# Product 2 by seven inner products in later gate/up, attention-output and down pairs, with h blocks handed on by a list of holders

## The chip, the core and the metric

The kernel runs on one core of one Trainium2 chip. The core has TensorE (matmuls into the eight banks of PSUM), VectorE and ScalarE (element-wise work on SBUF and PSUM), GpSimd (here only set-up and small powers) and SyncE, whose queue issues every DMA. The metric is the time of one execution on the device in microseconds, the median of the runs shown; lower is better.

## What is computed

One transformer-like block with a linear attention branch and a SwiGLU branch, for 2048 tokens of width 1024 and an inner width of 3584, all inputs in bf16:

```
xn  = layernorm(x)
q, k, v = split(xn @ wqkv)                      # 32 heads of 32
pq, pk  = phi(q), phi(k)                        # phi(t) = (t > 0 ? t + 1 : exp(t)) + 1e-6
kv, z   = sum_s pk v^T, sum_s pk                # per head
s   = ((pq @ kv) / (pq . z + 1e-6)) @ wo
g   = silu((silu(xn @ w_gate) * (xn @ w_up)) @ w_down)
out = x + s * g
```

## The kernel before

**Products.** A large matrix product is cut into 2 x 2 blocks and computed by the Strassen-Winograd scheme: seven block products (numbered 1 to 7) in place of eight, with sums of operand blocks made by VectorE beforehand and sums of results made afterwards. The stationary operand (a 128-column slice of weights or of tokens) has the combinations 5, 6, 7 and 3, made by `sums` (line 958); the moving operand has T1 to T4. One *set* (class `Set`, line 487) is one such scheme for one slice: its `step(m)` issues product m as wide matmuls (128 x 512 output, one PSUM bank), four of them where the half contraction is 512 long, fourteen in the down projection. Two sets that share their moving operand form a *pair* (class `Pair`, line 589).

Products 1 and 5 of a pair's two sets are computed together by a *joint* (class `Joint`, line 551): the same scheme applied once more inside, as seven inner products of narrow matmuls (128 x 256 output), two per inner product, seven in the down projection. A joint has four parts a, b, c, d; it takes two PSUM banks x and y, has ScalarE copy part of y to x and to a buffer of `q_ring`, and has VectorE add in parts b and c. Its end calls `put1` or `put5`: `put1` lets ScalarE copy the finished product 1 into a second bank, so that product 2 can accumulate onto one copy (result (0,0)) and product 6 onto the other; `put5` lets ScalarE copy product 5 into `s5_ring`. Product 6 is followed by a 512-wide VectorE add into a third bank, product 7 by one into `d_ring`. A first pair of a stage has no joint and runs `HEAD`, then `TAIL`; pairs with joints are interleaved with the rest of the pair before them in the fixed order `LINK` (line 607), issued by `feed` (line 610).

**Stages.** In order of time: layernorm, k and v with the kv sums (to about 100 us); the q, gate and up blocks in the order of `order` (line 1390), each 512 columns wide, for the token halves p = 0 and 1, one pair each (`q_pair`, `gu_pair`); after ("u", 3) four attention-output pairs (`s_pair`, line 1221); after ("u", 6) the down projection in four groups of 512 tokens (class `Group`, line 1308, and the loop at 1469), the first without joints. The element-wise product h goes through DRAM (`h_scr`) and comes back in blocks; a group's blocks (0,0), (0,1), (1,1), (1,0), their sums 5 and 6 (7 and 3 overwrite blocks), and the inner sums of joints 1 and 5 live in nine slots of 7 KB (`hslots`), handed on by callbacks `first` to `sixth` at named steps.

**Weights.** `wload` (line 968) brings a block of 1 MB into one of two slots of `raw_ring`, makes its sums into `cmb_ring`, and has `inner_stat` (line 995) make the inner sums of operands 1 and 5 into `in_ring`. `inner_move` (line 1022) makes the inner combinations of the moving operand once per token half.

**Order.** Everything above only records operations in a `Plan` (line 31) with the regions they read and write, in units of 256 bytes. `Plan.schedule` then orders them per engine by assumed costs and due times; TensorE may take an operation out of order among the next `WINDOW` = 6 matmul groups. `emit` writes the queues with semaphore waits. Each engine runs its queue in order.

Lines 229, 359, 369 and 372 are the helpers for matmuls, ScalarE operations, VectorE two-operand operations and DMA issue, so most groups of the profile carry these lines; tiles tell them apart (W: weights and inner sums; H: blocks of many kinds; X, P: the normalised tokens' halves; TM: small buffers; ps: PSUM).

Of the kernel before, what the change touches and what calls it, by code (L numbers as in the profile page):

```python
# [239 lines left out]
def build_kernel(nc, A_x, A_wqkv, A_wo, B_w_gate, B_w_up, B_w_down, out, WINDOW=6, NWARM=14, NPE=4, LEAD=12.0):  # L240
# [12 lines left out]
    with ExitStack() as es:  # L253
# [178 lines left out]
        d_ring = Ring(TM, 4 * KB, 2 * KB, 2)  # L432
# [5 lines left out]
        x_ring = Ring(W, 36 * KB, 2 * KB, 4)  # L438
        xn_ring = Ring(W, 0, 2 * KB, 2)
        xs_ring = Ring(W, 44 * KB, 4 * KB, 2)  # L440
# [46 lines left out]
        class Set:  # L487
# [4 lines left out]
            def __init__(self, ops, evac, dring):  # L492
                self.ops, self.evac, self.dring, self.direct = ops, evac, dring, None
# [19 lines left out]

            def put5(self, e):
                self.s5 = s5_ring.take()
                act([bank_r[e]], [self.s5.r], self.s5.ap(F32), ps[e][:, :], ACT.Identity)
                bfree(e)

            def step(self, m):
# [11 lines left out]
                elif m == 6:  # L531
                    self.grp(6, self.b, False)
                    self.c = balloc()
                    tt([bank_r[self.b], self.s5.r], [bank_r[self.c]], ps[self.c][:, :], ps[self.b][:, :],
                       self.s5.ap(F32), ALU.add)
                elif m == 7:
                    self.grp(7, self.b, False)
                    if self.direct is not None:
                        self.direct(1, 1, self.b, self.s5)
                        return  # L540
                    d = self.dring.take()
                    tt([bank_r[self.b], self.s5.r], [d.r], d.ap(F32), ps[self.b][:, :], self.s5.ap(F32), ALU.add)
# [46 lines left out]
        class Pair:  # L589
# [3 lines left out]
            def __init__(self, s0, s1, joint, at):  # L593
                self.sets, self.joint, self.at = (s0, s1), joint, at

            def do(self, w):
                if w[0] == "j":
# [4 lines left out]
                for fn in self.at.get(w, ()):  # L602
                    fn()

        HEAD = "1_0 5_0 1_1 2_0 5_1 6_0 2_1 6_1".split()
        TAIL = "7_0 3_0 7_1 4_0 3_1 4_1".split()
        LINK = "7_0 nj1a 3_0 7_1 nj1b nj5a 3_1 nj1c nj5b 4_0 nj1d nj5c 4_1 n2_0 nj5d n6_0 n2_1 n6_1".split()
        last_pair = [None]

        def feed(pair):  # L610

            prev = last_pair[0]
            if pair is None or not pair.joint:
                if prev is not None:
                    for w in TAIL:
                        prev.do(w)
# [3 lines left out]
            else:  # L620
                for w in LINK:
                    if w[0] == "n":
                        pair.do(w[1:])
                    elif prev is not None:
# [197 lines left out]
        def kv_set(u, w, stat):  # L822
# [16 lines left out]
            st = Set(ops, evac, d_ring)  # L839
# [118 lines left out]
        def sums(A, o, rd, wr):  # L958

            tt(rd, [wr[0]], o[0], A[0, 1], A[1, 1], ALU.add, True)  # L960
            tt(rd + [wr[0]], [wr[1]], o[1], o[0], A[0, 0], ALU.subtract, True)
            tt(rd, [wr[2]], o[2], A[0, 0], A[0, 1], ALU.subtract, True)
            tt(rd + [wr[1]], [wr[3]], o[3], A[1, 0], o[1], ALU.subtract, True)
# [4 lines left out]
        def wload(src, joint):  # L968
# [6 lines left out]
            cv = c.ap(FP16).rearrange("p (m w kt n) -> p m w kt n", m=4, w=2, n=128)  # L975
            cr = [c.sub(q * 2 * KB, 2 * KB).r for q in range(4)]
            sums({(k, i): v[:, :, 4 * k:4 * k + 4, i * 128:i * 128 + 128] for k in range(2) for i in range(2)},
                 [cv[:, q] for q in range(4)], [s.r], cr)

            def whole(m):  # L980
                if m in RAW_OF:
                    k, i = RAW_OF[m]
                    return v[:, :, 4 * k:4 * k + 4, i * 128:i * 128 + 128], s.r
                return cv[:, SUM_OF[m]], cr[SUM_OF[m]]

            def block(m):
                bl, r = whole(m)
                return (lambda k0, n, i: bl[:, i, k0:k0 + n, :]), r

            def stat(w, m):  # L990
                bl, r = whole(m)
                return [bl[:, w, q, :] for q in range(4)], r
            return stat, inner_stat(block, joint, 4, in_ring.take)

        def inner_stat(block, joint, kt, take):

            inner = {}
            for m in joint:
                bl, r = block(m)
                t = take()  # L1000
                n = kt // 2 * 256
                tv = t.ap(FP16, 0, 4 * n).rearrange("p (m kt n) -> p m kt n", m=4, n=128)
                tr = [t.sub(q * n, n).r for q in range(4)]
                A = {(k, i): bl(k * (kt // 2), kt // 2, i) for k in range(2) for i in range(2)}
                sums(A, [tv[:, q] for q in range(4)], [r], tr)
                inner[m] = (A, r, tv, tr)

            def jstat(m, k):
                A, r, tv, tr = inner[m]
                if k in RAW_OF:  # L1010
                    return [A[RAW_OF[k]][:, q, :] for q in range(kt // 2)], r
                return [tv[:, SUM_OF[k], q, :] for q in range(kt // 2)], tr[SUM_OF[k]]
            return jstat

        def xset(stat, w, xv, evac, dring):
# [4 lines left out]
            return Set(ops, evac, dring)  # L1020

        def inner_move(v, kt, at, raw=False, ms=(1, 5)):
# [3 lines left out]
            for m, places in zip(ms, at):  # L1026
# [3 lines left out]
                if raw and m == 1:  # L1030
# [9 lines left out]
        def in_places(arena, base, n):  # L1040
            return tuple(tuple((arena, base + (3 * m + q) * n) for q in range(3)) for m in range(2))
# [3 lines left out]
        def joint_of(jstat, xin, n, s0, s1):  # L1045
            def ops(m):
                def f(k):
# [4 lines left out]
            return {"1": Joint(ops(1), lambda w, b: (s0, s1)[w].put1(b)),  # L1052
                    "5": Joint(ops(5), lambda w, b: (s0, s1)[w].put5(b))}
# [17 lines left out]
        def q_load(s):  # L1071
            return wload(wqkv_v[:, :, s * 512:(s + 1) * 512], (1, 5))
# [10 lines left out]
        def q_pair(p, s, stats, at):  # L1083
            stat, jstat = stats

            def evac(w):
                def f(i, j, ap, r, bank):
                    g = 2 * (2 * s + w) + i
                    o, orr = pq_tile(p, g, j)
                    phi_evac(ap, r, o, orr, "ps" if bank is not None else "sb", i == 0)  # L1090
                return f
            s0, s1 = (xset(stat, w, XV[p], evac(w), d_ring) for w in range(2))
# [50 lines left out]
        def gu_load(k, n):  # L1143
            return wload((wg_v if k == "g" else wu_v)[:, :, n * 512:(n + 1) * 512], (1, 5))
# [13 lines left out]
        def gu_pair(p, kind, n, stats, at):  # L1158
# [38 lines left out]
            s0, s1 = (xset(stat, w, XV[p], (ev_g if kind == "g" else ev_u)(w), d_ring) for w in range(2))  # L1197
# [5 lines left out]
        def blocks(get, kt):  # L1203

            def block(m):
                ap, r = get(m)
                return (lambda k0, n, i: ap[:, k0:k0 + n, 128 * i:128 * i + 128]), r

            def stat(w, m):
                ap, r = get(m)  # L1210
                return [ap[:, q, 128 * w:128 * w + 128] for q in range(kt)], r
            return block, stat

        so_ring = Places([(TM, o * KB) for o in (8, 9, 12, 13)] + [(H, o * KB) for o in range(32, 40)], 1 * KB)
# [6 lines left out]
        def s_pair(g):  # L1221
            p, j0 = g // 2, g % 2
            A = {}
            for k in range(2):
                o = pq_off(p, k, j0)
                for i in range(2):
                    A[k, i] = (H.at(o, 4 * KB, FP16).rearrange("p (q t) -> p q t", t=512)[:, :, 256 * i:256 * i + 256],
                               H.reg(o, 4 * KB))
            c = ss_ring.take()
            cv = c.ap(FP16).rearrange("p (m q t) -> p m q t", m=4, t=256)  # L1230
            cr = [c.sub(q * 2 * KB, 2 * KB).r for q in range(4)]
            sums({q: a for q, (a, _) in A.items()}, [cv[:, q] for q in range(4)], [A[0, 0][1], A[1, 0][1]], cr)

            def get(m):
                return A[RAW_OF[m]] if m in RAW_OF else (cv[:, SUM_OF[m]], cr[SUM_OF[m]])
# [10 lines left out]
            s0, s1 = (xset(stat, w, MV, evac(w), d_ring) for w in range(2))  # L1246
            return Pair(s0, s1, joint_of(inner_stat(block, (1, 5), 4, in_ring.take), MIN, 2, s0, s1), {})
# [4 lines left out]
        def dblock(*at):  # L1252

            if len(at) == 1:
# [8 lines left out]
              "T4": dblock((W, 12 * KB), (H, 0))}  # L1263
# [21 lines left out]
        DAT = (tuple((W, q * 3584) for q in range(3)), ((W, 28 * KB), (W, 28 * KB + 3584), (W, 43 * KB)))  # L1285

        class Slots:
# [8 lines left out]
            def give(self, s):  # L1296
                self.free.append(s.k)

        hslots = Slots([(X, 0), (X, 7 * KB), (X, 14 * KB), (X, 21 * KB), (W, 20 * KB), (W, 36 * KB),
                        (H, 7 * KB), (H, 14 * KB), (H, 21 * KB)], 7 * KB)  # L1300
        g_ring = Places([(W, o * KB) for o in (47, 48, 49, 50)], 1 * KB)
        sl_ring = Places([(W, o * KB) for o in (51, 27, 35, 19)], 1 * KB)
        xo_ring = Places([(TM, 8 * KB), (TM, 9 * KB), (TM, 12 * KB), (TM, 13 * KB), (W, 11 * KB)], 1 * KB)
# [4 lines left out]
        class Group:  # L1308


            def __init__(self, g, cuts):
                self.g, self.cuts = g, cuts
                self.s, self.j = {}, {}

            def load(self, k, i):
                s = self.s[k, i] = hslots.take()
# [10 lines left out]
            def sum5(self):  # L1327
                self.s[5] = hslots.take()
                self.mk(self.s[5], self.s[0, 1], self.s[1, 1], ALU.add)

            def sum67(self):
                self.s[6] = hslots.take()
                self.mk(self.s[6], self.s[5], self.s[0, 0], ALU.subtract)
# [250 lines left out]
```

## Time and profile before

| | |
|---|---|
| median of 3 runs | 717.33 us (717.17 to 718.4) |
| the profiled execution's own time | 716.87 us |
| its span, first to last instruction | 715.1 us |
| granted TensorE clock | 0.998 |
| HBM read and written | 61.87 MB and 23.20 MB |

The span is the time in which the profile shows instructions; the execution's own time also has what lies before the first and after the last. Busy times of the page's first part are unions of the recorded intervals of an engine. A matmul's recorded end is modelled and overlaps the next one's start. A group's row gives its count, its busy time, the mean duration of one in ns, and the idle time of the engine ahead of it with what ended it.

### The profile page before, as it was taken

What the parts mean: (1) busy time and instruction counts of PE and PEld (TensorE: products, weight loads), DVE (VectorE), ACT (ScalarE), POOL (GpSimd) and SP (SyncE); (2) the same over time, 40 slices, a digit from 0 to 9 for tenths busy, and PEclk for the clock granted to TensorE, in tenths of its full rate; (3) what the DMA queues carried; (4) which work ended last, traced back from release to release, by engine and by line L of the source; (5) the groups of instructions that cost most, each with busy time, mean ns of one, the idle gap of its engine ahead of it and who ended that gap; (6) DMA issues with size and microseconds to landing.
All of it is one profiled execution on the core that took longest, in us unless ns stands there. A gap on an engine that the chain in (4) does not pass through costs nothing.

```text
span 715.1 us, 10861 instructions
## 1 busy us (share of the span) xinstructions
PE 705.0 (99%) x4035; PEld 385.8 (54%) x4064; DVE 528.0 (74%) x1181; ACT 407.4 (57%) x785; POOL 13.7 (2%) x35
## 2 busy tenths in 40 slices
PE   8999999999999999999999999999999999999997
PEld 3444445555555555555555555555554465565643
DVE  6998998676976797678998455957659994737442
ACT  4776655877876786679966665565662122121211
POOL 2111000000000000000000000000000000000000
PEclk9999999999999999999999999999999999999999
DMA  9443213113211330274225227554336646444412
GB/s 304 108 88 90 59 60 118 60 60 109 78 50 60 118 95 29 79 212 127 89 87 179 95 83 243 184 177 168 112 123 209 250 139 206 140 136 165 136 65 83
DMA packets 86869, 88.93 MB, mean 124 GB/s; under 512 B 17440, under 2 KB 82720, under 8 KB 86816
## 3 DMA queue, kind: packets, MB, share of 16 engines
q1 hardware_dynamic: 86816, 88.23, 39.0%
q8 instruction: 32, 0.52, 0.3%
q14 instruction: 21, 0.17, 0.1%
HBM read 61.87 MB, written 23.20 MB: 119 GB/s over the span
## 4 chain that ended last, share of the span: by engine, by line
PE 97%; DMA 1%; DVE 0%; SPq 0%; issue 0%; ACT 0%
PE ps L229 97%; DMA W<-in_A_x_dram 1%; SPq L372 0%; PE ps L236 0%; DVE stats L667 0%; DVE H L755 0%; ACT W L359 0%; DVE stats L671 0%; ACT ps L359 0%; DVE W L369 0%; DVE TM L369 0%; DVE mv L672 0%; DVE TM L754 0%; DVE veps L673 0%; DVE nmean L684 0%
## 5 line engine op out<-in xcount | busy, mean ns | idle before, releaser
L229 PE MATMUL ps<-P,W 128*128 128x512 f16 (+1 forms) x952 | 215.4, 350 | 0.0
L229 PE MATMUL ps<-X,W 128*128 128x512 f16 (+1 forms) x896 | 202.9, 351 | 0.0
L369 DVE TENSOR_TENSOR ps<-ps,TM 128x256 f32<-128x256 f32 (+1 forms) x246 | 130.5, 532 | 90.3 <-PE ps L229 64.2
L359 ACT ACTIVATE H<-ps 128x512 f16<-128x512 f32 (+2 forms) x225 | 133.5, 602 | 84.2 <-PE ps L229 83.7
L359 ACT ACTIVATE TM<-ps 128x512 f32<-128x512 f32 (+2 forms) x244 | 125.2, 531 | 33.3 <-PE ps L229 29.5
L229 PEld LDWEIGHTS ps<-P,W 128*128 128x128 f16 (+1 forms) x952 | 93.0, 98 | 73.8 <-ACT ps L359 0.3
L229 PEld LDWEIGHTS ps<-X,W 128*128 128x128 f16 (+1 forms) x896 | 87.4, 98 | 68.5 <-issue 0.2
L359 ACT ACTIVATE ps<-ps 128x512 f32<-128x512 f32 (+1 forms) x170 | 84.4, 496 | 62.2 <-PE ps L229 59.3
L369 DVE TENSOR_TENSOR W<-W 128x256 f16<-128x256 bf16 (+4 forms) x230 | 87.5, 418 | 25.9 <-ACT W L359 25.3
L369 DVE TENSOR_TENSOR H<-H 128x1024 f16<-128x1024 f16 (+3 forms) x143 | 85.7, 622 | 12.8 <-ACT H L359 8.1
L229 PE MATMUL ps<-H,X 128*128 128x512 bf16 (+3 forms) x376 | 80.0, 355 | 2.9 <-DVE nmean L684 0.9
L229 PE MATMUL ps<-W 128*128 128x256 f16 x444 | 78.5, 273 | 0.2
L229 PE MATMUL ps<-H,W 128*128 128x512 f16 (+3 forms) x365 | 76.8, 345 | 0.3
L229 PE MATMUL ps<-H 128*128 128x129 bf16 (+4 forms) x407 | 73.4, 315 | 0.4
L229 PEld LDWEIGHTS ps<-W 128*128 128x128 f16 (+1 forms) x444 | 43.2, 98 | 29.7 <-ACT TM L359 0.9
L229 PEld LDWEIGHTS ps<-H,X 128*128 128x128 f16 x388 | 37.3, 98 | 37.5 <-DVE H L755 1.2
L369 DVE TENSOR_TENSOR TM<-ps,TM 128x512 f32<-128x512 f32 x59 | 40.6, 688 | 21.0 <-PE ps L229 20.9
L229 PEld LDWEIGHTS ps<-H 128*128 128x128 f16 (+1 forms) x418 | 37.0, 98 | 31.8
L229 PEld LDWEIGHTS ps<-H,W 128*128 128x128 f16 x370 | 35.9, 98 | 32.0
L359 ACT ACTIVATE W<-ps 128x512 f16<-128x512 f32 x24 | 14.3, 597 | 54.5 <-PE ps L229 54.5
L369 DVE TENSOR_TENSOR H<-ps,TM 128x512 f16<-128x512 f32 (+1 forms) x35 | 24.1, 688 | 12.5 <-PE ps L229 12.1
L229 PE MATMUL ps<-W,H 128*128 128x512 f16 (+1 forms) x139 | 32.5, 368 | 0.0
(87 smaller groups left out, 461.1 us busy)
## 6 DMA issues: line engine op xcount, KB each, us to landing
h_scratch<-H SPq DMA_DIRECT2D x56, 256.0 KB, 2.2
W<-in_B_w_gate_dram SPq DMA_DIRECT2D x7, 1024.0 KB, 5.3
W<-in_B_w_up_dram SPq DMA_DIRECT2D x7, 1024.0 KB, 5.3
H<-in_B_w_down_dram SPq DMA_DIRECT2D x4, 1792.0 KB, 7.1
H<-h_scratch SPq DMA_DIRECT2D x7, 896.0 KB, 4.8
W<-in_A_x_dram SPq DMA_DIRECT2D x16, 256.0 KB, 3.2
H<-in_A_wqkv_dram SPq DMA_DIRECT2D x8, 512.0 KB, 8.1
H<-r_scratch SPq DMA_DIRECT2D x32, 128.0 KB, 3.2
```

The costliest lines, as they stand in the source:

```text
L229: last = h.matmul(o, l, r, start=st, stop=sp, skip_group_check=True)
L359: op = PL.op("act", reads, writes, lambda h: h.activation(o, i, func, **kw), nel(o) / 1200.0 + (0.055 if src == "ps" else 0.095))
L369: return dve(reads, writes, lambda h: h.tensor_tensor(o, a, b, op), nel(o), 1.92 if fast else 0.96)
```

## The change

Three things are changed together, and buffers, orders and the sums' places are rearranged around them.

*A third joint.* For later gate/up blocks (`THIRD`: token half 0 from ("g", 4) on, half 1 from ("g", 2) on), for all four attention-output pairs and for down groups 1 to 3, product 2 of the pair's two sets is also computed by a joint. Product 1 is then kept as a copy in SBUF (`keep1`, into `s1_ring`, which takes the place of `d_ring`) while its bank takes the products that accumulate on it; the finished product 2 is added to that copy by VectorE (`put2`), and the result (0,0) is evacuated from SBUF (or directly by that add, for up). Product 7's result is added in place into the `s5_ring` buffer.

```diff
+            def keep1(self, a):
+                self.b = a
+                self.s1 = s1_ring.take()
+                act([bank_r[a]], [self.s1.r], self.s1.ap(F32), ps[a][:, :], ACT.Identity)
+
+            def put2(self, b):
+                if self.direct is not None:
+                    self.direct(0, 0, b, self.s1)
+                    bfree(b)
+                    return
+                d = self.s1
+                tt([bank_r[b], d.r], [d.r], d.ap(F32), ps[b][:, :], d.ap(F32), ALU.add)
+                bfree(b)
+                self.evac(0, 0, d.ap(F32), d.r, None)
...
-            return {"1": Joint(ops(1), lambda w, b: (s0, s1)[w].put1(b)),
-                    "5": Joint(ops(5), lambda w, b: (s0, s1)[w].put5(b))}
+            js = {"5": Joint(ops(5), lambda w, b: (s0, s1)[w].put5(b))}
+            if 2 in xin or n == 7:
+                js["1"] = Joint(ops(1), lambda w, b: (s0, s1)[w].keep1(b))
+                js["2"] = Joint(ops(2), lambda w, b: (s0, s1)[w].put2(b))
+            else:
+                js["1"] = Joint(ops(1), lambda w, b: (s0, s1)[w].put1(b))
+            return js
...
+        THIRD = (("g", 4), ("g", 2))
+        S_THIRD = True
+        S_AT = 3
```

*Orders.* The interleaving of pairs gets one string per case (no third joint, both pairs with one, first with one, down), with leftovers of a pair done by `REST`; the planner's window goes from 6 to 10; the two q blocks stand next to each other; the steps at which the attention's m_build, recip and normalise parts are issued are listed one by one (`BUILD`, `RECIP`, `NORM`), as are the q results that ScalarE splits (`SPLIT`); the inner sums of operands 5 and 2 are made later, at named steps (`late`, `hook`).

```diff
-def build_kernel(nc, A_x, A_wqkv, A_wo, B_w_gate, B_w_up, B_w_down, out, WINDOW=6, NWARM=14, NPE=4, LEAD=12.0):
+def build_kernel(nc, A_x, A_wqkv, A_wo, B_w_gate, B_w_up, B_w_down, out, WINDOW=10, NWARM=14, NPE=4, LEAD=12.0):
...
-        LINK = "7_0 nj1a 3_0 7_1 nj1b nj5a 3_1 nj1c nj5b 4_0 nj1d nj5c 4_1 n2_0 nj5d n6_0 n2_1 n6_1".split()
+        LINK = "nj1a 7_0 3_0 nj1b 3_1 nj5a nj5b 7_1 nj1c 4_0 4_1 nj5c nj1d nj5d n6_0 n2_0 n2_1 n6_1".split()
+        LINK2 = ("nj1a nj5a 7_0 nj1b 4_0 3_1 j2d nj5b nj1c nj2a 7_1 nj2b nj5c n6_0 nj2c nj1d nj5d 4_1 n6_1 n3_0"
+                 ).split()
+        LINKD = "7_0 7_1 3_0 3_1 nj1a 4_0 nj1b 4_1 nj1c nj5a nj1d nj5b nj2a nj5c nj2b nj5d n6_0 nj2c n6_1 nj2d".split()
+        LINK1 = "7_0 nj1a 3_0 7_1 nj1b nj5a 3_1 nj1c nj5b 4_0 nj1d nj5c 4_1 nj5d n6_0 nj2a nj2b n6_1 nj2c nj2d".split()
+        REST = "j2a j2b j2c j2d 6_0 6_1 7_0 3_0 7_1 4_0 3_1 4_1".split()
...
-        raw_ring = Places([(W, o * KB) for o in (12, 20)], 8 * KB)
-        cmb_ring = Places([(W, o * KB) for o in (28, 36)], 8 * KB)
-        in_ring = Places([(W, o * KB) for o in (44, 46, 48, 50)], 2 * KB)
+        raw_ring = Places([(W, o * KB) for o in (18, 44)], 8 * KB)
+        cmb_ring = Places([(W, o * KB) for o in (26, 38)], 6 * KB)
+        in_ring = Places([(W, 32 * KB + o * 1536) for o in range(4)], 1536)
...
-        order = [("g", 0), ("u", 0), ("q", 0), ("g", 1), ("u", 1), ("q", 1)] + [
-            (k, n) for n in range(2, NPAIR // 2) for k in "gu"]
+        order = [("g", 0), ("u", 0), ("q", 0), ("q", 1), ("g", 1), ("u", 1), ("g", 2), ("u", 2), ("g", 3), ("u", 3), ("g", 4), ("u", 4), ("g", 5), ("u", 5), ("g", 6), ("u", 6)]
```

Sum 7 of a weight block (and of its inner operands) now overwrites the raw block it is made from, so the rings of sums are smaller, and reads and writes are tracked per 256-byte grain rather than per block.

*Holders.* In the down projection a slot is freed when the last of a listed set of users is done with it, and each group's list of loads and sums is tried again after every step of the group and of the one before it. There are six slots for blocks and two for inner sums.

```diff
+                self.todo = ["L00", "I1", "L01", "L11", "S5", "I5", "S7", "L10", "S6", "I2", "S3"]
...
+                self.hold = {"00": {"S6", "S7"}, "01": {"S5", "S7", "7_1"}, "11": {"S5", "4_1"}, "10": {"S3", "3_1"},
+                             "5": {"S6"}, "6": {"S3", "6_1"}}
...
+            def mark(self, t):
+                self.done.add(t)
+                for nm, h in list(self.hold.items()):
+                    if t in h:
+                        h.discard(t)
+                        if not h:
+                            (islots if nm[0] == "i" else hslots).give(self.s.pop(nm))
+                            self.hold.pop(nm)
...
+        def after(g, w):
+            G[g].mark(w)
+            for c in G[g:g + 2]:
+                c.pump()
```

More of the change, by code (lines that the diff above doesn't have):

```diff
@@ L532, in step @@
                     self.grp(6, self.b, False)
[L533 to L535 removed]
+                    self.sum5()
                 elif m == 7:
@@ L589, in build_kernel, with __init__ @@
         class Pair:
-            def __init__(self, s0, s1, joint, at):
-                self.sets, self.joint, self.at = (s0, s1), joint, at
+            def __init__(self, s0, s1, joint, at, down=False):
+                self.sets, self.joint, self.at, self.did, self.down = (s0, s1), joint, at, set(), down
             def do(self, w):
+                self.did.add(w)
                 if w[0] == "j":
@@ L614, in feed @@
                 if prev is not None:
-                    for w in TAIL:
-                        prev.do(w)
+                    for w in (REST if "2" in (prev.joint or ()) else TAIL):
+                        if w not in prev.did:
+                            prev.do(w)
                 if pair is not None:
@@ L620, in feed @@
             else:
-                for w in LINK:
+                third = [x is not None and "2" in (x.joint or ()) for x in (prev, pair)]
+                l2 = LINKD if pair.down else LINK2
+                link = LINK if not third[1] else l2 if third[0] else LINK1
+                early = REST[:6] if third == [True, False] else [w[1:] for w in l2] if third[0] else ()
+                for w in REST:
+                    if w in early and w not in prev.did:
+                        prev.do(w)
+                for w in link:
                     if w[0] == "n":
                         pair.do(w[1:])
-                    elif prev is not None:
+                    elif prev is not None and w not in prev.did and (w[0] != "j" or "2" in prev.joint):
                         prev.do(w)
@@ L974, in wload @@
             c = cmb_ring.take()
[L975 to L984, printed above, removed]
+            cv = c.ap(FP16).rearrange("p (m w kt n) -> p m w kt n", m=3, w=2, n=128)
@@ L990, in stat, with inner_stat, make @@
             def stat(w, m):
[L991 to L995, printed above, removed]
+                return [bl[m][:, w, q, :] for q in range(4)], rg[m]((w,), 0, 4)
+            return stat, inner_stat(block, joint, 4, in_ring.take, True, late)
+        def inner_stat(block, joint, kt, take, inplace=False, late=()):
             inner = {}
-            for m in joint:
[L999 to L1006, printed above, removed]
+            h = kt // 2
+            def make(m):
+                t = slots[m]
+                n = h * 256
+                ns = 3 if inplace else 4
+                tv = t.ap(FP16, 0, ns * n).rearrange("p (m kt n) -> p m kt n", m=ns, n=128)
+                o = [tv[:, q] for q in range(ns)]
+                wr = [t.sub(q * n, n).r for q in range(ns)]
+                A, R = {}, {}
+                for k in range(2):
+                    for i in range(2):
+                        A[k, i], R[k, i] = block(m)(k * h, h, i)
+                if inplace:
+                    d = A[0, 1]
+                    o.insert(2, d.bitcast(FP16) if d.dtype != FP16 else d)
+                    wr.insert(2, R[0, 1])
+                sums(A, R, o, wr)
+                inner[m] = (A, R, o, wr)
+            slots = {m: take() for m in joint}
+            for m in joint:
+                if m not in late:
+                    make(m)
@@ L1016, in ops, with hook, xset @@
+            jstat.late = {m: partial(make, m) for m in late}
+            return jstat
+        def hook(at, late, steps):
+            at = {w: list(fs) for w, fs in at.items()}
+            for m, w in steps.items():
+                if m in late:
+                    at.setdefault(w, []).append(late[m])
+            return at
+        def xset(stat, w, xv, evac):
             def ops(m):
@@ L1196, in direct @@
                 return f
-            s0, s1 = (xset(stat, w, XV[p], (ev_g if kind == "g" else ev_u)(w), d_ring) for w in range(2))
+            s0, s1 = (xset(stat, w, XV[p], (ev_g if kind == "g" else ev_u)(w)) for w in range(2))
             if kind == "u":
@@ L1245, in evac @@
                 return f
-            s0, s1 = (xset(stat, w, MV, evac(w), d_ring) for w in range(2))
-            return Pair(s0, s1, joint_of(inner_stat(block, (1, 5), 4, in_ring.take), MIN, 2, s0, s1), {})
+            s0, s1 = (xset(stat, w, MV, evac(w)) for w in range(2))
+            ms = (1, 5, 2) if S_THIRD else (1, 5)
+            jstat = inner_stat(block, ms, 4, in_ring.take, True, [m for m in late if m in ms])
+            s_late.update(jstat.late)
+            return Pair(s0, s1, joint_of(jstat, MIN, 2, s0, s1), {})
         GB = 14 * KB
@@ L1460, in build_kernel @@
         G = [Group(g, ((0, NPAIR),) if g else ((0, 12), (12, 14))) for g in range(4)]
-        for k, i in ((0, 0), (0, 1), (1, 1), (1, 0)):
-            G[0].load(k, i)
-        G[0].sum5()
-        G[0].sum67()
+        G[0].pump()
         feed(None)
```

311 lines of the change are left out of this document (189 added, 122 removed).

## The prediction

> **What bounds the kernel now.** I began with the page's first and fourth parts: what each engine is busy with, and the chain of work that ended last.
>
> ```profile
> span 715.1 us, 10861 instructions
> PE 705.0 (99%) x4035; PEld 385.8 (54%) x4064; DVE 528.0 (74%) x1181; ACT 407.4 (57%) x785; POOL 13.7 (2%) x35
> PE 97%; DMA 1%; DVE 0%; SPq 0%; issue 0%; ACT 0%
> ```
>
> TensorE is busy for 705 of 715.1 us and 97% of the last chain is matmuls. Matmul ends are modelled, so I asked the list of waits for what TensorE ever waited for:
>
> ```profile
> PE ps L229 <- POOL ident L412: 1.4, 1, 1.4
> PE ps L229 <- DVE nmean L684: 0.9, 1, 0.9
> PE ps L229 <- DMA H<-in_A_wqkv_dram: 0.7, 1, 0.7
> PE ps L229 <- ACT X L359: 0.5, 1, 0.5
> PE ps L229 <- ACT ps L359: 0.2, 1, 0.2
> ```
>
> 3.7 us in all. The chain in order of time (start, us, what) puts the last of them, for ScalarE, at 36 us:
>
> ```profile
> 36.19 0.59 ACT ps L359
> 36.78 0.05 issue
> 36.83 8.41 PE ps L229 x44
> ...
> 160.04 385.16 PE ps L229 x2281
> ```
>
> After it come only matmuls and breaks of 0.05 us until 710.3 us, and no product of this change computes before 100 us. So the time goes with the number and width of matmuls. The price of one is the distance between starts, not the modelled duration. It is read from runs of one width in the timeline (start, duration, count at the end):
>
> ```profile
> 408.68 3.62 PE L229 MATMUL ps<-X,W 128*128 128x512 f16 x16
> 412.13 0.38 PE L229 MATMUL ps<-P,W 128*128 128x256 f16 x2
> ...
> 626.80 0.93 PE L229 MATMUL ps<-W,X 128*128 128x256 f16 x7
> 627.56 0.93 PE L229 MATMUL ps<-H,X 128*128 128x256 bf16 x7
> 628.33 0.93 PE L229 MATMUL ps<-W,X 128*128 128x256 f16 x7
> 629.09 0.93 PE L229 MATMUL ps<-H,W 128*128 128x256 f16 x7
> 629.86 1.67 PE L229 MATMUL ps<-W,H 128*128 128x512 f16 x7
> ```
>
> Sixteen 512-wide ones take 412.13 - 408.68 = 3.45 us, 0.2156 us each. Twenty-eight 256-wide ones take 629.86 - 626.80 = 3.06 us, 0.1093 us each. A narrow one costs 51% of a wide one.
>
> **The change part by part.**
>
> *Matmuls.* In a pair with the new joint "2", the two sets' eight wide matmuls of product 2 (four each) give way to seven inner products of two 256-wide matmuls: minus 8 wide, plus 14 narrow. The pairs: gate/up from ("g", 4) for token half 0 (6 pairs) and from ("g", 2) for half 1 (10), and 4 attention-output pairs, 20 in all: minus 160 wide, plus 280 narrow. In the last three down groups a product has 14 k-blocks: minus 28 wide, plus 49 narrow each, together minus 84 and plus 147. Sum: minus 244 wide and plus 427 narrow, and the instruction lists of the two programs differ by just that. 427 x 0.1093 - 244 x 0.2156 = 46.7 - 52.6 = -5.9 us. Were a narrow one exactly half a wide one it would be -6.6, and nothing in the rows allows more.
>
> Against halving matmuls stands a rule of the Trainium skill, "TensorE: Matmul & The Clock Gate", section "Wait — 56ns, not 53.3ns?": a fixed ≈2.5 ns per matmul on top of N/2.4 GHz, whatever its width. By it the sum would be (427 - 244) x 2.5 ns - 15,616 fewer columns / 2.4 GHz, about -6.0 us, an estimate; the rows, which already contain such a cost, say -5.9 and are used.
>
> *VectorE.* It gets 176 more instructions (1183 to 1359 in the programs): per new pair two 256-wide adds of joint 2, two 512-wide adds in put2, and four small sums per inner operand. They sit on an engine that may run beside TensorE. Mean durations by form, then starts in a stretch where the engine is never idle:
>
> ```profile
> L369 DVE TENSOR_TENSOR ps<-ps,TM 128x256 f32<-128x256 f32 x152 | 65.1, 430 | 36.0 <-PE ps L229 35.3
> L369 DVE TENSOR_TENSOR TM<-ps,TM 128x512 f32<-128x512 f32 x59 | 40.6, 688 | 21.0 <-PE ps L229 20.9
> L369 DVE TENSOR_TENSOR W<-W 128x1024 f16<-128x1024 bf16 x48 | 31.7, 683 | 0.0
> L369 DVE TENSOR_TENSOR W<-W 128x256 f16<-128x256 f16 x80 | 21.3, 284 | 0.0
> ```
>
> ```profile
> 357.86 0.43 DVE L369 TENSOR_TENSOR ps<-ps,TM 128x256 f32<-128x256 f32 x1
> 358.19 1.02 DVE L369 TENSOR_TENSOR H<-H 128x512 f16<-128x512 bf16 x2
> ...
> 362.03 0.28 DVE L369 TENSOR_TENSOR W<-H 128x256 f16<-128x256 f16 x1
> 362.23 0.68 DVE L369 TENSOR_TENSOR W<-H,W 128x1024 f16<-128x1024 f16 x1
> 362.83 0.70 DVE L369 TENSOR_TENSOR ps<-ps,TM 128x512 f32<-128x512 f32 x1
> 363.44 0.28 DVE L369 TENSOR_TENSOR W<-W,H 128x256 f16<-128x256 f16 x1
> ```
>
> Each starts before its predecessor's record ends: 0.33, 0.20, 0.60 and 0.61 us apart where the records last 0.43, 0.28, 0.68 and 0.70. The distances are what the queue costs. An attention-output pair then needs six joint adds (2.0), six 512-wide adds (3.6: two each of sum5, m7, put2), four sums of 1024 (2.4) and twelve of 256 (2.4): 10.4 us, against 32 x 0.2156 + 42 x 0.1093 = 11.5 us of matmuls. A late gate/up pair needs 2.0 + 3.6, half of a weight block's 4.8 and, for up, 2.4 of products: 9.2 on average against 11.5. A down group has 40 us of matmuls and about 26 of VectorE. It fits, but tightly round the attention output, where deferred sums come on top. How TensorE fares under such a load is seen before the change (stretch, length, then busy us of PE, PEld, DVE, ACT):
>
> ```profile
> 345.00:387.00 42.00, 42.00 (x246) 23.95 (x245) 39.48 (x99) 32.44 (x66) 0.00 (x0) 1.00 0.43 138
> 387.00:524.00 137.00, 137.00 (x801) 78.26 (x800) 88.53 (x190) 85.73 (x180) 0.00 (x0) 1.00 0.44 144
> ```
>
> VectorE 94% busy, TensorE never idle. If that cover goes, the excess shows. I added the distances along VectorE's new queue, placing each instruction by the matmul it waits for: 69.4 us where TensorE has 68.4 (around the attention output), and 59.2 us in 57.0 (down group 0 into group 1, with the weight sums). Were none of that deferrable, 1.0 + 2.2 = 3.2 us would reach TensorE; the lower bound is 0. I take 0.4, near 0, since the row nearest in kind (345 to 387) shows 0.
>
> *Waits inside the joint.* The third joint adds three round trips TensorE, VectorE or ScalarE, TensorE per pair. What one takes is read from the end of the kernel, where nothing overlaps:
>
> ```profile
> 708.58 1.67 PE L229 MATMUL ps<-H 128*128 128x512 f16 x7
> 710.29 0.60 ACT L359 ACTIVATE W<-ps 128x512 f16<-128x512 f32 x1 [2.42 <-PE ps L229]
> 710.92 0.42 DVE L369 TENSOR_TENSOR W<-W 128x512 f16<-128x512 f16 x1 [2.14 <-ACT W L359]
> ```
>
> Each hand-over is 0.03 to 0.04 us. A narrow matmul's record lasts 0.273 us (0.164 beyond its slot), so a 256-wide add returns after 0.164 + 0.04 + 0.43 + 0.03 = 0.66 us if its queue is free. In the new order the tightest place has six narrow matmuls (0.66 us) between release and use, seven others eight, the rest ten or more: no loss alone. Behind one 1024-wide sum such an add comes 0.6 us later, and what is late next is the joint's following group and whatever matmuls stand behind it, since TensorE takes its queue in order. The same price holds for the planner's wider look-ahead (10 groups for 6), the new interleaving, and the q pairs put next to each other: they add no matmul, and are costed at nothing under the cover above, with 0.6 us for each displaced add as the other bound.
>
> *ScalarE* trades 46 PSUM-to-PSUM and 32 evacuating copies for 35 copies into TM, 46 narrow ones and 16 evacuations from TM; it was 85.73 of 137.00 us busy in the second stretch above, 63%, so nothing.
>
> *Loads.* The DMAs are the same 308. Weight slots of the later blocks are released about 9.0 us of matmuls ahead of the first matmul that needs the new block's sums; before, 8.4 to 11.5. The page has
>
> ```profile
> W<-in_B_w_gate_dram SPq DMA_DIRECT2D x7, 1024.0 KB, 5.3
> ```
>
> so 3.7 us stay for the first sums at 0.60, where 8.4 was enough. The h blocks of the down groups are now taken when a list of holders empties, the tightest 10.6 us of matmuls ahead of use; such a block's landing would have to double to be late. Nothing, with about 1 us per block as the upper bound.
>
> *Sum against the profiled execution.* 715.1 - 5.9 + 0.4 = 709.6 us of span. That execution's own time was 716.87, 1.8 us outside the span, so 711.4; the median of the runs is 717.33, 0.46 higher: **711.8 us**.
>
> **The rivals.**
>
> (1) *VectorE's backlog reaches TensorE a little.* The 3.2 us of excess and some displaced adds: 1.5 to 4 us of waits, 713 to 716. For it: six stretches of 11.4 us in a row with 10.1 to 12.8 us of VectorE. Against: 345 to 387.
>
> (2) *VectorE decides; slower.* Place: the joints of the 20 new pairs. Price: one add per pair behind one 1024-wide sum, 0.6 us, is 12 us, so 717.3 - 5.9 + 12 = 723.4; from 0.3 us per pair on the gain is gone. The same side results if a VectorE instruction costs its whole record: an attention-output pair is then 6 x 0.43 + 6 x 0.69 + 4 x 0.68 + 12 x 0.28 = 12.8 us against 11.5, which with the late gate/up pairs' 11.2 and their neighbours' deferred sums makes 8 to 12 us of waits, 720 to 723. The starts 0.60 apart speak against that half, the unbroken 42.00 us against both. The Trainium skill, "VectorE: DVE Perf Modes", section "The DRAIN you can't avoid", says that the next op does not start until the pipe is empty, though it grants that one that isn't held starts earlier; by it this rival would hold, and the trace disagrees with 0.60 for 0.68.
>
> (3) *The gain is lost to late loads.* Nine weight blocks late by about 0.6 us each: near 717. For it: slots are held longer, since 4_1 now comes near the end of the link. Against: 8.4 us was enough.
>
> (4) *The change does not do what it says.* Excluded for the matmuls by the instruction lists.
>
> **How the numbers follow.** Forecast (710.5 to 713) 0.64, rival 1 0.15, rival 3 with other small losses 0.07, rival 2 0.14 (0.02 of it for the whole-record half). A measurement here tells 0.2%, 1.4 us, from no change: faster is below 715.9, which the first two hold, 0.79; 715.9 to 718.8 is 0.07; slower 0.14. The range goes from 710.5 (the full 6.6 with no wait gives 710.7) to 716.0 (rival 1's end) and holds 0.79.
>
> **What would show it.** Right: 4249 instructions in TensorE's program and a busy time near 699; no TensorE wait after 40 us above a few tenths in sum; VectorE's busy share from 74% to about 84%; the group TM<-ps,TM 128x512 grown from 59 to 89. Wrong: TensorE waits on VectorE at ps of some us between 320 and 390 or 520 and 580 (rival 1), everywhere in the 20 pairs (rival 2), or VectorE sums waiting on DMA W<-in_B_w_up_dram and TensorE behind them (rival 3). A narrow matmul slower than 0.1093 in runs of two would cost the sum itself.

## The result, and the profile after

| | kernel before | changed kernel |
|---|---|---|
| median | 717.71 us (717.17 to 718.4, 6 runs) | 712.02 us (711.88 to 713.56, 6 runs) |
| the profiled execution's own time | 716.87 us | 711.92 us |
| its span | 715.1 us | 710.2 us |

The ratio is 0.9925, 95% interval 0.9913 to 0.9938: faster by 5.7 us.

The page of the changed kernel, its first and fourth parts:

```profile
span 710.2 us, 11461 instructions
PE 700.8 (99%) x4247; PEld 403.4 (57%) x4247; DVE 590.3 (83%) x1357; ACT 416.1 (59%) x815; POOL 12.8 (2%) x35
PE 92%; DVE 5%; DMA 1%; SPq 0%; ACT 0%; issue 0%
```

VectorE went from 74% to 83%, and it now has 5% of the last chain, which it did not have. What TensorE waited for, in us in total, times, longest:

```profile
PE ps L229 <- POOL ident L412: 1.4, 1, 1.4
PE ps L229 <- DVE nmean L718: 0.8, 1, 0.8
PE ps L229 <- DMA H<-in_A_wqkv_dram: 0.7, 1, 0.7
PE ps L236 <- DVE veps L707: 0.5, 1, 0.5
PE ps L229 <- DVE ps L369: 0.5, 2, 0.3
PE ps L229 <- ACT X L359: 0.5, 1, 0.5
```

Of these only 0.3 us (one of the two at ps) come after the first 100 us. They come where VectorE, which makes the sums, is never idle, as the stretches of the changed kernel show (stretch, length, busy us of PE, PEld, DVE, ACT and POOL, granted clock, DMA share, GB/s):

```profile
345.00:387.00 42.00, 41.69 (x270) 26.00 (x268) 42.00 (x110) 28.48 (x61) 0.00 (x0) 1.00 0.36 120
387.00:524.00 137.00, 137.00 (x884) 86.34 (x883) 117.06 (x274) 93.62 (x199) 0.00 (x0) 1.00 0.47 150
524.00:581.00 57.00, 57.00 (x307) 29.80 (x305) 53.65 (x92) 15.67 (x31) 0.00 (x0) 1.00 0.53 170
```

VectorE is busy for 42.00 of 42.00 us round the attention output (345 to 387 us), and TensorE idles there for 0.31 us. The stop itself is longer than this idle time (start, duration, count at the end):

```profile
354.67 0.38 PE L229 MATMUL ps<-H 128*128 128x256 f16 x2
355.37 0.39 PE L229 MATMUL ps<-W 128*128 128x256 f16 x2 [0.31 <-DVE ps L369]
```

Two narrow matmuls take 0.22 us from start to start, and these took 355.37 - 354.67 = 0.70, so TensorE lost 0.48 us. Idle columns and lists of waits count only from the last recorded end. That end lies 0.164 us behind the matmul's slot (0.273 us recorded for a narrow one, 0.109 from start to start), so they show each stop too short by that much, and a shorter stop not at all. Below, "stops" are therefore added up from start to start: each distance between two starts, less 0.2158 us for a wide and 0.1092 us for a narrow matmul, the means of the undisturbed distances in these traces.

The chain of the changed kernel in order of time (start, us, what) shows the same place from the other side:

```profile
127.74 206.07 PE ps L229 x1266
333.81 0.02 issue
333.84 0.69 DVE TM L369
...
354.97 0.35 DVE ps L369
355.32 0.05 issue
355.37 348.31 PE ps L229 x2160
```

From 334 to 355 us the work that ended last ran through VectorE, one operation behind the other, and through matmuls for all the rest from 37 to 703.7 us.

Where the 5 us of span came from is read off two marks in each timeline, the last transposes before the gate blocks' bulk and the last matmuls. The kernel before (its last matmuls start at 708.58, shown above):

```profile
126.69 0.61 PE L236 MATMUL ps<-ident,H 128*128 128x128 f16 x8
```

The changed kernel:

```profile
127.13 0.61 PE L236 MATMUL ps<-ident,H 128*128 128x128 f16 x8
...
703.50 1.67 PE L229 MATMUL ps<-H,X 128*128 128x512 f16 x7
```

Between these two marks 708.58 - 126.69 = 581.89 us became 703.50 - 127.13 = 576.37: 5.52 us less, waits included. Ahead of the first mark the changed kernel lost 0.44 us, behind the last 0.18 (710.2 - 703.50 against 715.1 - 708.58). That makes 4.9 us of span; the medians differ by 0.8 more, because the profiled execution of before, 716.87, lies below all six runs of the table.

### The profile page after: what moved, and what is told of

Its sections match the earlier page's. It is cut to its first block, busy times and chain, and to the rows that moved or that the text cites. A ratio compares the mean times of both kernels' runs of the same rounds, so it can differ in the third digit from the quotient of the medians.

```text
span 710.2 us, 11461 instructions
## 1 busy us (share of the span) xinstructions
PE 700.8 (99%) x4247; PEld 403.4 (57%) x4247; DVE 590.3 (83%) x1357; ACT 416.1 (59%) x815; POOL 12.8 (2%) x35
## 4 chain that ended last, share of the span: by engine, by line
PE 92%; DVE 5%; DMA 1%; SPq 0%; ACT 0%; issue 0%
PE ps L229 92%; DVE H L369 2%; DMA W<-in_A_x_dram 1%; DVE W L369 1%; DVE ps L369 1%; SPq L372 0%; DVE TM L369 0%; DVE H L789 0%; PE ps L236 0%; DVE stats L701 0%; DVE stats L705 0%; ACT W L359 0%; ACT X L359 0%; DVE TM L788 0%; DVE mv L706 0%
## 5 line engine op out<-in xcount | busy, mean ns | idle before, releaser
L369 DVE TENSOR_TENSOR ps<-ps,TM 128x256 f32<-128x256 f32 (+1 forms) x292 | 145.9, 511 | 51.8 <-PE ps L229 48.5
L359 ACT ACTIVATE TM<-ps 128x512 f32<-128x512 f32 (+2 forms) x302 | 151.9, 528 | 54.8 <-PE ps L229 53.1
L359 ACT ACTIVATE H<-ps 128x512 f16<-128x512 f32 (+2 forms) x192 | 112.6, 603 | 48.2 <-PE ps L229 46.6
L369 DVE TENSOR_TENSOR W<-W 128x256 f16<-128x256 f16 (+4 forms) x272 | 99.6, 402 | 19.2 <-ACT W L359 15.0
L229 PE MATMUL ps<-H,W 128*128 128x512 bf16 (+3 forms) x504 | 110.0, 355 | 0.2 <-DVE ps L369 0.2
L359 ACT ACTIVATE ps<-ps 128x256 f32<-128x256 f32 (+1 forms) x147 | 65.3, 444 | 66.1 <-PE ps L229 63.5
L369 DVE TENSOR_TENSOR H<-H 128x1024 f16<-128x1024 f16 (+6 forms) x149 | 85.8, 592 | 7.7 <-ACT H L359 6.3
L369 DVE TENSOR_TENSOR TM<-ps,TM 128x512 f32<-128x512 f32 x89 | 61.1, 686 | 21.0 <-PE ps L229 20.5
L229 PE MATMUL ps<-H 128*128 128x256 f16 (+4 forms) x390 | 55.0, 273 | 0.0
L359 ACT ACTIVATE H<-TM 128x512 f16<-128x512 f32 x58 | 36.5, 630 | 12.4 <-DVE TM L369 12.3
L229 PE MATMUL ps<-W,H 128*128 128x256 f16 (+1 forms) x230 | 42.9, 317 | 0.0
L369 DVE TENSOR_TENSOR H<-ps,TM 128x512 f16<-128x512 f32 (+1 forms) x51 | 34.8, 685 | 5.9 <-PE ps L229 5.5
```

The lines of the kernel that those rows point to most:

```text
L229: last = h.matmul(o, l, r, start=st, stop=sp, skip_group_check=True)
L359: op = PL.op("act", reads, writes, lambda h: h.activation(o, i, func, **kw), nel(o) / 1200.0 + (0.055 if src == "ps" else 0.095))
L369: return dve(reads, writes, lambda h: h.tensor_tensor(o, a, b, op), nel(o), 1.92 if fast else 0.96)
```

## The experiments

Each kernel was compared with the kernel before in runs of its own; the medians of that one were 717.65 to 717.73. "Between the marks" is the distance used above. In each expectation the "theory" is that the matmuls set the time and VectorE's work hides beside them; the "rival" is another reading of the gain. By the intervals of the ratios a median here is good to about 0.9 us. TensorE's busy time is not compared, since the records of some executions lack 22 to 29 matmuls.

The stops between the marks are 0.8 us in the changed kernel and about 0.3 in the kernel before. Less its stops, the distance between the marks of every kernel below differs from that of the changed kernel by the exchanged matmuls at the two undisturbed distances, to about 0.1 us.

### One part of the new joint taken away at a time

Gate/up without it, but for block ("u", 6):

```diff
-        THIRD = (("g", 4), ("g", 2))
+        THIRD = (("u", 6), ("u", 6))
```

> The third joint starts only at ("u", 6), so 14 of the 16 gate/up pairs do product 2 with wide matmuls again. If the matmuls alone set the time (theory): 14 x (8 x 0.2156 - 14 x 0.1093) = +2.7 us on the changed kernel's 712.0, 714.7. If the new joints cost about what they save, in VectorE waits, and the gain comes from the new orders (rival): 712.0 or less, since VectorE loses 34 us of queue.

Measured 715.01 us (ratio 0.9959, 0.9948 to 0.9971), 3.0 us above the changed kernel, 0.21 per pair. Between the marks 579.17, 2.80 more. The theory holds here (2.7 us expected), and the rival falls: VectorE is less busy where the joints are gone, 93.69 us for 117.06 from 387 to 524, and nothing was won by it:

```profile
387.00:524.00 137.00, 137.00 (x810) 79.01 (x808) 93.69 (x204) 89.38 (x185) 0.00 (x0) 1.00 0.45 149
```

Attention output without it:

```diff
-        S_THIRD = True
+        S_THIRD = False
```

> The four attention-output pairs lose the third joint. Theory: +4 x 0.195 = +0.8 us of matmuls, less the 0.5 us that TensorE waits for VectorE there in the changed kernel: 712.3. Rival (VectorE, which is busy for 42.00 of 42.00 us in this stage, costs more than the trace shows): 711 or less.

713.93 us (0.9946, 0.9934 to 0.9958): 1.9 above, where the theory said 0.3 and the rival less than nothing. Both are wrong, the rival by its sign. (Of the 0.5 us of waits that the theory takes off, only 0.3 lie in this stage; 0.2 lie in the first 100 us.) Between the marks it is 578.02, 1.65 more: 0.8 for the matmuls, and TensorE's stops did not go but grew, by 0.9. The list has a wait of 0.5 for ScalarE at 361 us and, already in the gate/up pairs behind, one of 0.3 for VectorE at TM at 415. Pairs without the third joint between pairs with it run other interleavings (`LINK1`, `LINK`), and the same flag gives the attention output's results more buffers (`so_ring`). Which of these makes the stops was not followed up. The first mark stood 0.75 later too (see the last section).

Down groups without it:

```diff
-            if 2 in xin or n == 7:
+            if 2 in xin:
...
+                else:
+                    self.todo.remove("I2")
...
-                self.hold["10"] |= {"I2", "j2d"} if self.joint else {"2_1"}
+                self.hold["10"] |= {"2_1"}
```

> The three later down groups lose the third joint; the list of holders stays. Theory: +3 x (28 x 0.2156 - 49 x 0.1093) = +2.0 us, 714.0. Rival (the down gain comes from the holders, or is paid back in sums): 712.0 to 712.5.

714.23 us (0.9953, 0.994 to 0.9965), 2.2 above; between the marks 2.09 more against 2.04 computed. So the joints' matmuls account for it, and nothing is left for the list of holders, which stayed.

All three edits in one kernel:

> No third joint but in the two pairs of ("u", 6); orders, window, rings and the list of holders stay as in the changed kernel. Theory: the orders are worth nothing, since TensorE had no wait to lose: 717.7 - 0.4 = 717.3, a ratio of 0.9995 to the kernel before. Rival (orders and holders bring a part): 716 or less. Other rival (they cost, and the joints bring more than counted): 718.5 or more.

717.8 us (0.9999, 0.9991 to 1.0008); between the marks 581.82, where the kernel before has 581.89. New orders, rings, holders and window, with no third joint but in the two pairs of ("u", 6): no change. Those two pairs alone should save 0.4 us, so the rest may cost as much; the interval of 0.6 us to either side does not tell. The gain is the joints'.

### The planner's window

```diff
-... out, WINDOW=10, NWARM=14, NPE=4, LEAD=12.0):
+... out, WINDOW=6, NWARM=14, NPE=4, LEAD=12.0):
```

> The changed kernel with the planner's window back at 6 matmul groups; the same matmuls in another order from the first stage on. Theory (VectorE hides as long as its queue is ahead of TensorE): with less freedom some joint adds come late, above all where VectorE is full; 712 to 714. Rival (the wider window is what makes the third joints fit): 715 or more. Other rival (it does nothing): 712.0.

Measured 718.67 us (1.0019, 1.0011 to 1.0028): the same 4247 matmuls take 6.6 us longer, and the whole gain is gone. The rival holds: the wider window is what makes the third joints fit. TensorE's waits in this kernel, those that the changed kernel does not have or has smaller:

```profile
PE ps L229 <- DVE H L369: 2.3, 1, 2.3
PE ps L229 <- ACT ps L359: 2.0, 5, 0.5
PE ps L229 <- DMA H<-in_A_wqkv_dram: 1.6, 1, 1.6
PE ps L229 <- DVE H L789: 1.0, 1, 1.0
PE ps L229 <- DVE ps L369: 0.6, 1, 0.6
```

and two of its stretches:

```profile
345.00:387.00 42.00, 40.93 (x261) 24.86 (x260) 42.00 (x109) 26.52 (x58) 0.00 (x0) 1.00 0.35 116
524.00:581.00 57.00, 54.51 (x289) 28.38 (x291) 52.27 (x88) 18.06 (x36) 0.00 (x0) 1.00 0.50 160
```

VectorE is as full as in the changed kernel, 42.00 of 42.00, but TensorE now idles 1.07 us beside it instead of 0.31, and 2.49 instead of 0 at the change to the down projection, where one wait of 2.28 us stands at 551.6: a matmul group that waits for VectorE's add of a bank into H, which ran among the down projection's sums. Between the marks (582.43) lie 6.06 us more. The stops there are 6.9 us in place of 0.8, which is all of it; the list has 4.7 of them, for VectorE's operations of L369 (2.3 and 0.6) and for ScalarE's copies at ps (1.8; its other 0.2 lie ahead of the first mark).

Is the window worth something by itself? The kernel before with 10:

```diff
-... out, WINDOW=6, NWARM=14, NPE=4, LEAD=12.0):
+... out, WINDOW=10, NWARM=14, NPE=4, LEAD=12.0):
```

> The kernel before with the window at 10, nothing else. Theory: it has no TensorE wait after 37 us to remove, so 717.7, no change. Rival (the wider window is worth something by itself): 716 or less.

718.99 us (1.0017, 1.0008 to 1.0025): not faster, but slower by 1.3. The rival falls, and so does the theory's "no change". Where it lies is clear from the marks of this kernel:

```profile
129.26 0.61 PE L236 MATMUL ps<-ident,H 128*128 128x128 f16 x8
...
711.16 1.67 PE L229 MATMUL ps<-H 128*128 128x512 f16 x7
```

711.16 - 129.26 = 581.90, the same as before to 0.01 us. The profiled executions differ by 2.6 us, and these are lost ahead of the first mark, where TensorE now waits 1.0 for VectorE at veps and 1.6 for the first weights in place of 0.7. So the window buys nothing here, where TensorE has nothing to wait for between the marks. By the medians it costs 1.3 us in the start; the landing of the first weights differs between executions anyway (last section), so the 2.6 us are not all the window's.

Two more sizes on the changed kernel, WINDOW=14 and WINDOW=8:

> The changed kernel with a window of 14 matmul groups. With 6 it took 718.7. If freedom of order is what keeps the joint adds early: 712.0 or a little less (TensorE has only 0.5 us of waits left there). If 10 is merely an order that happened to suit: 713 or more.

712.25 us (0.9927, 0.9915 to 0.994): the same. Between the marks 576.24, 0.13 less than with 10; ahead of them 1.7 us more, with waits of 2.7 in place of 0.7 for the first weights.

> The changed kernel with a window of 8. If freedom of order is what counts, between 10 and 6: 713 to 717. If not, anything outside.

714.03 us (0.9953, 0.9941 to 0.9966): between, as expected. Over 6, 8, 10 and 14 the distance between the marks is 582.43, 578.48, 576.37 and 576.24: the benefit ends at 10.

### More work on VectorE

One VectorE operation more, which changes no value, ahead of each put2, in the attention output or in the late gate/up pairs:

```diff
             def put2(self, b):
+                if self.twice:
+                    tt([bank_r[b], self.s1.r], [self.s1.r], self.s1.ap(F32), self.s1.ap(F32), self.s1.ap(F32), ALU.max)
```

`twice` is set for the sets of the attention-output pairs alone:

> The changed kernel with one more VectorE operation ahead of each put2 of the four attention-output pairs (the maximum of the s1 buffer with itself, 512 wide, about 0.60 us): 8 operations, 4.8 us of queue, in the stage where VectorE is busy for 42.00 of 42.00 us. Theory (there VectorE is full, and what is added reaches TensorE once the deferrable sums are used up): 2 to 5 us more, 714 to 717. Rival (the records overlap and VectorE has room): 712.0 to 712.5.

713.27 us (0.9947, 0.9934 to 0.9961), 1.25 more (1.15 between the marks), on average 0.16 per added operation of 0.60.

and for the gate/up blocks from 4 on alone:

> The same operation ahead of each put2 in the gate/up pairs of blocks 4 to 6: 24 operations, 14.4 us of queue, where VectorE is busy for 117.06 of 137.00 us. Theory (there is room for it): less than 0.7 us more, up to 712.7. Rival (each add lies on the joint's own way back to TensorE, so that it costs whatever the engine's load): 24 x 0.2 to 0.6 us, 717 or more.

714.53 us (0.9957, 0.9945 to 0.997), 2.5 more (2.33 between the marks), on average 0.10 per operation. Both lie between the theory and its rival. The stretches of the kernel with the eight operations, and TensorE's new waits in the kernel with the 24:

```profile
345.00:387.00 42.00, 41.59 (x267) 25.59 (x265) 42.00 (x108) 28.09 (x60) 0.00 (x0) 1.00 0.35 116
387.00:524.00 137.00, 136.38 (x881) 85.95 (x880) 120.49 (x283) 92.55 (x199) 0.00 (x0) 1.00 0.46 150
```

```profile
PE ps L229 <- DVE ps L369: 1.1, 3, 0.7
PE ps L229 <- ACT TM L359: 0.9, 2, 0.5
```

In the first, the full stage could not take more: VectorE's busy time in the next stretch grew by 3.43 of the 4.8 us (117.06 to 120.49), and TensorE's stops grew by 0.3 us in the full stage and by 0.8 in the next. So "full" is not a wall as long as sums can be put off.

In the second, there was room, and it cost nonetheless. An average share below 100% does not mean that an added operation is free: a sixth of its queue time reached TensorE. But it did not come as 0.10 us each. Nearly all of it is three stops, two of them alike, of which these are the first and the last:

```profile
454.81 0.60 PE L229 MATMUL ps<-W 128*128 128x256 f16 x4
455.88 0.39 PE L229 MATMUL ps<-X,W 128*128 128x512 f16 x1 [0.47 <-ACT TM L359]
...
596.58 0.93 PE L229 MATMUL ps<-H 128*128 128x256 f16 x7
598.17 0.94 PE L229 MATMUL ps<-H 128*128 128x256 f16 x7 [0.67 <-DVE ps L369]
```

From start to start they cost 1.07 - 4 x 0.109 = 0.63 us, the same again at 502 us, and 1.59 - 7 x 0.109 = 0.83 us: 2.1 of the 2.33 us between the marks. Two wait for ScalarE's copies into TM, for which TensorE did not wait before, and the third stands in the down projection, where no operation was added. The planner orders everything anew around the added work, so whether the price is the operations' or the new order's stays open.

### Going further in the same direction

```diff
-        THIRD = (("g", 4), ("g", 2))
+        THIRD = (("g", 2), ("g", 2))
```

> The third joint for token half 0 starts at ("g", 2) too: 4 more pairs. Theory (VectorE has room between 160 and 320 us, 135.29 of 160.00 busy): 4 x 0.195 = 0.8 us less than the changed kernel, 711.2. Rival (each further pair costs more in late adds than it saves, as the 24 added operations of e9 cost 0.1 us each): 712.0 or more.

713.78 us (0.9944, 0.9932 to 0.9957). 4 pairs more cost 1.8 us instead of saving 0.8. Its stretches:

```profile
160.00:320.00 160.00, 159.84 (x1012) 93.62 (x1010) 138.30 (x338) 126.79 (x262) 0.00 (x0) 1.00 0.32 98
345.00:387.00 42.00, 40.98 (x261) 24.57 (x260) 42.00 (x106) 27.12 (x57) 0.00 (x0) 1.00 0.36 120
```

The smaller part of the loss is where the pairs were added, the larger part afterwards, where VectorE was full already: 1.02 us of idle TensorE from 345 to 387 in place of 0.31. The idle times show less than half of it. TensorE's stops grew by 0.5 us from 160 to 320 (0.20 to 0.74) and by 1.8 from 345 to 387 (0.50 to 2.27), 2.3 in all, and with the 0.8 us of matmuls saved that gives the 1.51 more between the marks (577.88). A reading is that what VectorE puts off earlier has no room in the full stage.

```diff
-        THIRD = (("g", 4), ("g", 2))
+        THIRD = (("g", 1), ("g", 1))
```

> The third joint starts at ("g", 1) for both halves: 8 more pairs, next to the q blocks' work and the normalisation. Theory: 1.6 us less, 710.5. Rival: 712 or more, with new TensorE waits between 200 and 320 us.

713.78 us (0.995, 0.9936 to 0.9964): the 1.6 us of matmuls saved are outweighed, with 1.04 us idle in the attention output again and 0.46 between 160 and 320. The stops of the full stage are no larger than with half as many added pairs (2.3 us in both), so they do not grow with the work that could be put off; that reading is argued, not shown, and the order that the planner made of this stage is its rival. The change's own set of pairs is the best of those tried, and no kernel here is faster than the changed one.

## Why the prediction was right

*The sum of matmuls* (-5.9 us). Between the marks 5.52 us went although the stop at 355 us added 0.48, so the matmuls gave 6.0. That the list of waits has only 0.3 us would have made it 5.8. Taking the parts away gave 0.21 us per pair (0.195 computed) and 0.74 per down group (0.68). A run of narrow matmuls in the changed kernel has the price that was used, 28 in 671.66 - 668.61 = 3.05 us, 0.109 each:

```profile
668.61 0.93 PE L229 MATMUL ps<-H 128*128 128x256 bf16 x7
669.37 0.93 PE L229 MATMUL ps<-H,X 128*128 128x256 f16 x7
670.14 0.93 PE L229 MATMUL ps<-W 128*128 128x256 f16 x7
670.90 0.93 PE L229 MATMUL ps<-H 128*128 128x256 f16 x7
671.66 0.60 PE L229 MATMUL ps<-H,W 128*128 128x256 bf16 x4
```

*VectorE's cover* (0.4 us of waits, bounds 0 and 3.2). After the first 100 us the list has 0.3 us, and the stop behind it cost 0.5. The stretch named as the tightest, around the attention output, is where it was. The second, between down groups 0 and 1, lost nothing. The groups grew as counted:

```profile
L369 DVE TENSOR_TENSOR ps<-ps,TM 128x256 f32<-128x256 f32 x198 | 82.6, 425 | 33.8 <-PE ps L229 32.6
L369 DVE TENSOR_TENSOR TM<-ps,TM 128x512 f32<-128x512 f32 x89 | 61.1, 686 | 21.0 <-PE ps L229 20.5
```

46 more of the first, 30 more of the second, and a busy share of 83% for the 84% named.

*Waits inside the joint* (no loss alone). Held. The price for a displaced add, up to 0.6 us, held as a bound on the average, with eight and 24 more operations at 0.16 and 0.10 each; but in the second kernel it came as three single stops of 0.63, 0.63 and 0.83.

*Orders and window at nothing.* The number was right and the reason too short. Without the joints they are worth nothing that can be seen (717.8), and the window alone costs (718.99 in the kernel before). With the joints, the window is what makes the cover: at 6 the same sum would have been off by 6.6 us, and the kernel would have been slower than the one before (718.67), as rival 2 has it, without one VectorE operation more. It would not have been rival 2's 720 to 723, nor stops everywhere in the new pairs, and 1.8 us of the waits would have been for ScalarE. The prediction asked whether VectorE has the time, and its operations are the same in both kernels; it should also have asked in which order they are done.

*Loads* (nothing). No wait of TensorE for gate, up, down or h blocks is in the list.

*Rival 2*, its whole-record half, expected 8 to 12 us of waits; TensorE lost 0.5. The prediction lets the Trainium skill, "VectorE: DVE Perf Modes", section "The DRAIN you can't avoid", speak for this rival. The same section lets an instruction that is not held start earlier, which agrees with the trace's 0.60 us between starts for a record of 0.68.

*What the sum had no term for* is the start: 0.44 us in the profiled executions. *What was named as a sign and missed* is TensorE's busy time, 700.8 for "near 699". The trace of before has 4064 weight loads, one for each matmul, but only 4035 matmuls, so 705.0 was too small to start from; how much of the 1.8 us that explains stays open. The median came within 0.2 us of 711.8, and part of that is luck: the forecast started from 717.33, the median of three runs, and that of all six is 0.38 us higher.

## What to carry to other kernels

Where TensorE is busy all the time and its list of waits is empty, count matmuls by the distance between their starts; here the answer was good to a few tenths of a microsecond. Measure its stops by these distances too, since the list of waits begins late: with the four further pairs the idle times showed less than half of the loss. Then ask of the engine that takes over the work not only whether its queue distances add up to less than TensorE's time in each stage, but also in which order it gets to it: here the same operations in another order cost as much as the change gained. Look at a full stage also when work is moved to the engine in the stages ahead of it: with four further pairs most of the loss stood there.

## What the runs showed of the hardware

VectorE was busy for 42.00 of 42.00 us, over 110 operations, with TensorE losing 0.5 us beside it. The first weights' landing differs between executions: the changed kernel and the one without the attention output's joint have the same instructions on every engine until well past 100 us, yet TensorE waited 0.7 us for H<-in_A_wqkv_dram in one and 1.6 in the other. On a change of 0.8% such a start alone is a sixth of the effect, which is why the distance between two marks was read beside the medians.
